# Combine weights transposed four tiles at a time and spread to their rows by DMA, S's columns made in pairs: an attention, soft-MoE and MLP kernel

## The chip, the core and the metric

The kernel runs on one core of a Trainium2 chip. The metric is device time in microseconds (us) of one execution, lower is better. The engines are named as the profile names them: PE is the matmul engine, PEld its weight loads, DVE the vector engine, ACT the scalar engine, POOL GpSimd, SP the engine whose queue issues the DMAs.

## The reference

Three layers follow each other, all in float32. What is computed, cut to what matters:

```python
# 1 attention: q, k, v are 8 batches x 8 heads x 576 x 64; keys and values are averaged in groups of 8 (72 left)
attn = softmax(q @ k_p.T / 8) ; x = (attn @ v_p), laid out as 4608 tokens x 512
# 2 soft MoE, 8 experts of 4 slots each (32 slots)
logits = x @ phi                               # 4608 x 32
d = softmax(logits, axis=0); slot_input = d.T @ x
slot_out[e] = relu(slot_input[e] @ w1[e]) @ w2[e]   # w1 512x1024, w2 1024x512 per expert
c = softmax(logits, axis=1)                    # the combine weights
y = c @ slot_out                               # 4608 x 512
# 3 MLP
g = s * relu(y @ w_in) ** 2 + b                # w_in 512 x 2048
out = g @ w_out                                # w_out 2048 x 512
```

The w_in and w_out that arrive are 64-bit floats, which the kernel turns into float32 itself.

## The kernel before

The program is one straight line of instructions per engine, in the order in which the source issues them. No engine overtakes its own queue, and waits are set by the data. SP issues every DMA, also in order.

**Attention, 0 to about 200 us.** The 36 tiles of 128 tokens pass through a hand-written pipeline. Its end leaves the logits in four tiles `L_t[pr]`, one for each pair of batches, 128 tokens x (9 tiles of tokens + 2 spare) x 32 slots.

**Experts, about 202 to 250 us.** A loop over `EORD` takes the 32 weight pieces of 1 MB (numbered 0 to 31 here; the loop's `n_`): w1 pieces write `l1` (L944), w2 pieces write `so_ps` (L952), each with 8 narrow matmul passes. After the last w1 piece of a half (pieces 7 and 21) `hidden` copies `l1` to SBUF on ACT (first half) and DVE (second half, L922), PE sums it one piece later (`hps`, L926), and ACT makes `h1z` from it (L928), which the w2 pieces read. `done(key, keep)` gives a piece's buffer back, or keeps it as scratch, and `pump` issues the next loads, strictly in the order of `loads`. `WIPOS` and `WOPOS` say ahead of which piece the first load of w_in and of w_out stands in that order; those two go to a `raw` buffer.

After each piece `step_convs` advances the generators in `convs` by one step and starts one more from `todo`. In `todo` stand:

- `combine(pr)`, the softmax over slots, in place in `L_t[pr]`;
- 20 `combine_t(pr, t0, n)`, which make the combine weights' transpose `cT` for two tiles of tokens (or one): ACT and DVE write the weights twice as a rounded high part and a low part into `cs`, PE transposes (L903), ACT copies to `cT`. A tile of `cT` has 128 rows: 32 slots x (high, low, high, low) parts;
- the first conversions: `conv_wi(0)`, `conv_wi(1)`, `conv_wo(0)`, `conv_wo(1)`. Each converts a 128 x 512 block by `narrow`: five DVE operations (L823 to L833), one on ACT (L835), two on POOL (L836, L837).

**The start of the MLP.** After piece 31, PE runs two filler matmuls on `cT` (`busy`, L980), the slots' outputs are transposed (`sot`), and a list `OPS` makes the first two column blocks of S = slot_out @ w_in (`s_a` writes `sps`, `s_b` spreads it to `Sw_t[f]` as high and low parts), the first hidden tiles (`st_h`, L1021), and their parts `gh` and `gl` (`st_g`). For step 0 both halves of `gh` are cast on DVE (L1048).

**The MLP, about 258 to 697 us.** 96 steps, each with 18 matmuls of 128 x 512 (`st_o`, L1078) and 2 of 128 x 384 (`st_h`). Conversions and, for f = 2 to 15, one `s_a` and one `s_b` each are threaded in between.

Of the kernel before, what the change touches and what calls it, by code (L numbers as in the profile page):

```python
# [56 lines left out]
def kernel(  # L57
# [793 lines left out]
    def s_a(f, ps):  # L851

        t = t_wi.pop(f)
        for kc in range(4):
# [1 line left out]
        sps = cv.tile([128, 128], F32, tag="sps", name="sps", bufs=2)
        sps_t[f] = sps
        nc.scalar.copy(out=sps, in_=ps[:, 0:128])

    def s_b(f, ps):  # L860

        nc.tensor.matmul(out=ps, lhsT=selrep.rearrange("p r s -> p (r s)"), rhs=sps_t.pop(f), start=True, stop=True)
        nc.scalar.copy(out=Sw_t[f], in_=ps)
        nc.vector.tensor_tensor(out=Sw_t[f][64:128], in0=ps[64:128], in1=Sw_t[f][64:128].bitcast(F32), op=ALU.subtract)  # L864
# [29 lines left out]
    def combine_t(pr, t0, n):  # L894
        cs = cv.tile([128, 2, 2, 2, 32], F32R, tag="cs", name="cs", bufs=2)[:, 0:n]
        cb = L_t[pr][:, 1 + t0:1 + t0 + n].unsqueeze(2).to_broadcast([128, n, 2, 32])
        nc.scalar.copy(out=cs[:, :, :, 0, :], in_=cb)
        nc.vector.tensor_tensor(out=cs[:, :, :, 1, :], in0=cb, in1=cs[:, :, :, 0, :].bitcast(F32), op=ALU.subtract)
        yield
        yield  # L900
        ps = ps_x.tile([128, 512], F32, tag="sx", name="ct")
        for i in range(n):
            nc.tensor.transpose(  # L903
                out=ps[:, 128 * i:128 * i + 128],
                in_=cs[:, i].rearrange("p a b s -> p (a b s)").bitcast(F32),
                identity=ident,
            )
# [295 lines left out]
```

## Time and profile before

| | |
|---|---|
| median of 3 runs | 707.07 us (705.78 to 707.13) |
| the profiled execution | 707.28 us |
| its span, first to last instruction | 705.2 us |
| PE busy | 661.7 us (94%) |
| DVE, ACT, POOL busy | 489.2, 410.2, 291.5 us |
| mean granted TensorE clock | 0.973 |
| DMA | 88.87 MB |

The profiled execution lies 0.21 us above the median and 2.1 us above its own span. The shares are averages over stages with different limits, so a stage is to be read in its own window: from 300 us on PE is busy in nearly every microsecond at a granted clock of 1.00; between 200 and 262 us the clock moves between 0.50 and 1.00 and other engines end PE's waits.

### The profile page before, as it was taken

Reading aid. Unit: us, or ns where it says so; the run is one execution under the profiler, and the core shown is the slowest. Engines: PE = TensorE matmul, PEld = TensorE weight load, DVE = VectorE, ACT = ScalarE, POOL = GpSimd, SP = SyncE. Lnnn points to the kernel's source line nnn. Section 1 sums busy time; section 2 is a strip of 40 time slices with the busy share of each in tenths; the row PEclk is TensorE's granted clock in tenths of the full one; section 3 lists DMA queues with packets and bytes.
Section 4 is the critical chain, followed back from the end, with each engine's and each line's share of the span. In section 5 each row is a group of like instructions: output and inputs, shape, how many; then the busy total and the mean of one; then the engine's idle time right before and its main releaser. Section 6 shows DMA issues by size and latency. Waiting matters only on the chain.

```text
span 705.2 us, 11293 instructions
## 1 busy us (share of the span) xinstructions
PE 661.7 (94%) x4354; PEld 518.3 (73%) x4354; DVE 489.2 (69%) x771; ACT 410.2 (58%) x714; POOL 291.5 (41%) x221
## 2 busy tenths in 40 slices
PE   7777989898989879999999999999999999999997
PEld 6665768677743348778888878788788788888885
DVE  6879777677582686888667788886765674556443
ACT  3664666665323347885666656666565666555552
POOL 3866466422100353543243335444141433999000
PEclk9998999999689989999999999999999999999999
DMA  8999276626669931011030110301100000222222
GB/s 290 383 344 311 109 240 241 239 72 229 248 237 384 361 142 61 1 59 60 2 118 2 60 59 1 119 1 61 60 0 1 1 0 1 89 91 88 92 91 89
DMA packets 41317, 88.87 MB, mean 126 GB/s; under 512 B 6960, under 2 KB 15152, under 8 KB 41264
## 3 DMA queue, kind: packets, MB, share of 16 engines
q1 hardware_dynamic: 41264, 88.16, 36.1%
q8 instruction: 34, 0.56, 0.3%
q14 instruction: 19, 0.16, 0.1%
HBM read 78.71 MB, written 9.44 MB: 125 GB/s over the span
## 4 chain that ended last, share of the span: by engine, by line
PE 77%; DVE 14%; ACT 4%; issue 1%; DMA 1%; POOL 1%; SPq 1%; DVEq 0%; ACTq 0%; POOLq 0%
PE o L1078 53%; PE h L1021 5%; PE sc L389 3%; PE l L944 3%; DVE S L398 2%; DVE mx L396 2%; PE so_ps L952 2%; DVE sm L407 2%; PE w L440 1%; DMA ring<-in_q_dram 1%; PE w L606 1%; ACT S L406 1%; PE w L359 1%; PE w L583 1%; PE ct L903 1%
## 5 line engine op out<-in xcount | busy, mean ns | idle before, releaser
L1078 PE MATMUL o<-whi,gh 128*128 128x512 f32 x576 | 229.1, 398 | 2.5 <-DVE gh L1048 2.5
L1078 PE MATMUL o<-whi,gl 128*128 128x512 f32 x576 | 225.1, 391 | 1.0 <-DVE gl L1049 1.0
L1078 PE MATMUL o<-wlo,gh 128*128 128x512 f32 x576 | 225.2, 391 | 0.0
L1030 ACT ACTIVATE r<-h 128x768 f32<-128x768 f32 x95 | 77.2, 813 | 151.9 <-PE h L1021 148.0
L1049 DVE TENSOR_TENSOR gl<-r,gh 128x768 fp32r<-128x768 f32 (+1 forms) x97 | 114.5, 1181 | 63.2 <-ACT gh L1038 62.8
L1091 DVE SCALAR_TENSOR_TENSOR part<-o,sb_t,part 128x512 f32<-128x512 f32 x144 | 99.6, 744 | 50.3 <-PE o L1078 47.8
L1078 PEld LDWEIGHTS o<-whi,gh 128*128 128x128 f32 x576 | 108.6, 188 | 23.9 <-issue 5.6
L1078 PEld LDWEIGHTS o<-wlo,gh 128*128 128x128 f32 x576 | 108.4, 188 | 24.0
L1078 PEld LDWEIGHTS o<-whi,gl 128*128 128x128 f32 x576 | 108.7, 189 | 21.6 <-DVE gl L1049 2.9
L836 POOL TENSOR_TENSOR fr<-fr,xp 128x512 f32<-128x512 f32 x28 | 41.0, 1464 | 182.4 <-ACT fr L835 160.3
L1031 ACT ACTIVATE r<-r 128x768 f32<-128x768 f32 x95 | 80.4, 847 | 3.0
L1038 ACT CAST gh<-r 128x768 fp32r<-128x768 f32 x95 | 79.5, 837 | 2.4
L427 POOL TENSOR_TENSOR P<-S,rs 128x576 f32<-128x576 f32 x32 | 37.3, 1166 | 72.7 <-DVE rs L410 38.0
L1172 POOL TENSOR_TENSOR part<-part,wsum 128x512 f32<-128x512 f32 x36 | 53.3, 1521 | 10.5 <-ACT wsum L1166 10.5
L1021 PE MATMUL h<-cT,S 128*128 128x384 f32 x192 | 48.8, 336 | 0.5 <-DVE S L864 0.5
L837 POOL TENSOR_TENSOR th<-th,fr 128x512 f32<-128x512 f32 x28 | 43.0, 1537 | 2.2
L1021 PEld LDWEIGHTS h<-cT,S 128*128 128x128 f32 x192 | 35.9, 188 | 8.1 <-DVE S L864 0.7
L407 DVE TENSOR_REDUCE sm<-S 128x8 f32<-128x584 f32 x36 | 27.3, 758 | 19.8 <-ACT S L406 19.7
L389 PE MATMUL sc<-kb,qT 128*128 128x144 f32 x256 | 39.7, 301 | 0.2 <-ACT qT L361 0.2
L396 DVE TENSOR_REDUCE mx<-sc 128x8 f32<-128x576 f32 x36 | 26.4, 734 | 15.5 <-PE sc L389 12.9
L389 PEld LDWEIGHTS sc<-kb,qT 128*128 128x128 f32 x256 | 35.5, 201 | 0.7 <-ACT qT L361 0.5
L406 ACT ACTIVATE S<-S 128x576 f32<-128x576 f32 x36 | 24.6, 682 | 19.5 <-DVE S L398 19.2
(211 smaller groups left out, 899.4 us busy)
## 6 DMA issues: line engine op xcount, KB each, us to landing
ring<-in_moe_w_dram SPq DMA_DIRECT2D x14, 1024.0 KB, 7.3
x<-in_moe_w_dram SPq DMA_DIRECT2D x13, 1024.0 KB, 9.2
raw<-in_moe_w_in_dram SPq DMA_DIRECT2D x8, 1024.0 KB, 5.5
raw<-in_moe_w_out_dram SPq DMA_DIRECT2D x8, 1024.0 KB, 4.8
out_dram<-part SPq DMA_DIRECT2D x32, 256.0 KB, 2.5
ring<-in_q_dram SPq DMA_DIRECT2D x7, 1024.0 KB, 13.4
ring<-in_v_dram SPq DMA_DIRECT2D x9, 768.0 KB, 11.4
ring<-in_k_dram SPq DMA_DIRECT2D x7, 768.0 KB, 7.7
```

The costliest lines, as they stand in the source:

```text
L389: nc.tensor.matmul(out=sc[:, i // 2, 2 * KP * (i % 2):2 * KP * (i % 2) + 2 * KP], lhsT=qT[:, i, :], rhs=kb[:, H * bb + 4 * (j % 2) + i, :] ...
L407: nc.vector.tensor_reduce(out=sm, in_=S, axis=AX.X, op=ALU.add)
L836: nc.gpsimd.tensor_tensor(out=fr, in0=fr, in1=xp, op=ALU.mult)
L837: nc.gpsimd.tensor_tensor(out=th if dst is None else dst, in0=th, in1=fr, op=ALU.add)
L1021: nc.tensor.matmul(out=h[x][:, 0:384] if i == 0 else h[:, x, 0:384], lhsT=Sw_t[f], rhs=cT(c, 384), start=True, stop=True)
L1030: nc.scalar.activation(out=r, in_=h[:, :, 0:384], func=ACTF.Relu)
L1031: nc.scalar.activation(out=r, in_=r, func=ACTF.Square)
L1038: nc.scalar.copy(out=gh_t[i], in_=r)
L1049: nc.vector.tensor_tensor(out=gl[:, x], in0=r[:, x], in1=gh[:, x].bitcast(F32), op=ALU.subtract)
L1078: nc.tensor.matmul(out=o_t[tt], lhsT=l[:, x, 128 * c:128 * c + 128], rhs=r, start=(fi == 0 and n == 0), stop=(fi == GROUPS[g] - 1 and n == 2),
L1091: nc.vector.scalar_tensor_tensor(out=p, in0=o_t[tt], scalar=sb_t[:, 0:1], in1=p, op0=ALU.mult, op1=ALU.add)
L1172: nc.gpsimd.tensor_tensor(out=p, in0=p, in1=wsum, op=ALU.add)
```

## The change

- The four tiles of logits become one, `L_all`, 128 x 11 x 4 x 32, so that for one index of a tile of tokens the four pairs' 32 slots lie side by side: 128 columns. `L_t[pr]` is now a strided view of it.
- `combine_t` is one generator. It transposes the nine blocks of 128 columns in groups of 4, 4 and 1; ACT writes the rounded high part back in place into `L_all`, DVE writes the low part into a fourth kept buffer, `kept[3]`. Then 16 DMAs of 32 rows x 1152 columns carry, for each pair, high, low, high, low to the four row groups of `cT`.
- It is started at piece 15, the first conversions at pieces 18, 19, 23 and 24 (table `BEHIND`). `WIPOS` goes from 22 to 25, `WOPOS` from 25 to 26. A fourth buffer is kept, and three of the four (pieces 7, 8, 9) from earlier pieces than before.
- S's columns are made for two f at a time where both are converted (`ready`): `s_a` and `s_b` take a pair, with one copy, one matmul of 256 columns, one cast and one subtract. f = 4 and f = 7, the last of groups of three, stay single, and so do f = 0 and 1.
- For step 0 the first half of `gh` is cast on ACT, the second on DVE. `wsum`'s first two steps come after both `wlo`.

```diff
-WIPOS, WOPOS = 22, 25
+WIPOS, WOPOS = 25, 26
+BEHIND = {15: "c", 18: "i0", 19: "i1", 23: "o0", 24: "o1"}
...
-    L_t = [cpool.tile([128, 11, 32], F32, name=f"L{i}") for i in range(NPR)]
+    L_all = cpool.tile([128, 11, NPR, 32], F32, name="L")
+    L_t = [L_all[:, :, i, :] for i in range(NPR)]
...
-    def s_a(f, ps):
-
-        t = t_wi.pop(f)
-        for kc in range(4):
-            nc.tensor.matmul(out=ps[32 * kc:32 * kc + 32, 0:128], lhsT=sot[:, kc, :], rhs=t[:, kc, :], start=True, stop=True)
...
+    def s_a(fs, ps):
+
+        for i, f in enumerate(fs):
+            t = t_wi.pop(f)
+            for kc in range(4):
+                nc.tensor.matmul(
+                    out=ps[32 * kc:32 * kc + 32, 128 * i:128 * i + 128], lhsT=sot[:, kc, :], rhs=t[:, kc, :], start=True, stop=True
+                )
+        n = 128 * len(fs)
...
+        nc.scalar.copy(out=sps_t[fs[0]], in_=ps[:, 0:n])
+
+    def s_b(fs, ps):
+
+        n, f = 128 * len(fs), fs[0]
+        nc.tensor.matmul(out=ps[:, 0:n], lhsT=selrep.rearrange("p r s -> p (r s)"), rhs=sps_t.pop(f), start=True, stop=True)
...
-    def combine_t(pr, t0, n):
-        cs = cv.tile([128, 2, 2, 2, 32], F32R, tag="cs", name="cs", bufs=2)[:, 0:n]
...
+    def combine_t():
+
+
+        x0 = 0
+        for j0, n in ((0, 4), (4, 4), (8, 1)):
+            x = 128 * n
+            Lc = L_all[:, 1 + j0:1 + j0 + n].rearrange("p j r s -> p (j r s)")
+            ps = ps_x.tile([128, 512], F32, tag="sx", name="ct")
+            for i in range(n):
+                nc.tensor.transpose(out=ps[:, 128 * i:128 * i + 128], in_=Lc[:, 128 * i:128 * i + 128], identity=ident)
+            nc.scalar.copy(out=Lc.bitcast(F32R), in_=ps[:, 0:x])
+            yield
+            nc.vector.tensor_tensor(out=kept[3][:, x0:x0 + x].bitcast(F32R), in0=ps[:, 0:x], in1=Lc, op=ALU.subtract)
+            x0 += x
+        hl = (L_all[:, 1:10].rearrange("p j r s -> p (j r s)"), kept[3][:, 0:x0])
+        for pr in range(NPR):
+            dst = cT(9 * pr * 128, x0).bitcast(F32)
+            for r in range(4):
+                nc.sync.dma_start(out=dst[32 * r:32 * r + 32], in_=hl[r % 2][32 * pr:32 * pr + 32])
...
-        done(key, 3 if n_ > 9 else int(n_ > 2))
+        done(key, 4 if n_ > 6 else int(n_ > 2))
...
+        if n_ in BEHIND:
+            x, f = BEHIND[n_][0], int(BEHIND[n_][1:] or 0)
+            todo.appendleft(conv_wi(f) if x == "i" else islice(wo_[f], 2) if x == "o" else combine_t())
...
+        if i == 0:
+            nc.scalar.copy(out=gh[:, 0], in_=r[:, 0])
+            nc.vector.tensor_copy(out=gh[:, 1], in_=r[:, 1])
         for x in (slice(0, 1), slice(1, 2)) if i == 0 else (slice(0, 2),):
-            if i == 0:
-                nc.vector.tensor_copy(out=gh[:, x], in_=r[:, x])
             nc.vector.tensor_tensor(out=gl[:, x], in0=r[:, x], in1=gh[:, x].bitcast(F32), op=ALU.subtract)
...
+    def ready():
+
+        if not t_wi:
+            return ()
+        f = min(t_wi)
+        g, i = GOF[f]
+        if i + 1 == GROUPS[g]:
+            return (f,)
+        return (f, f + 1) if f + 1 in t_wi else ()
```

Three places where instructions change their order. First DVE's queue around piece 21. `cs` are the old high and low parts, L the logits, `si_all` the copy of `l1` that `hps` needs, and `ring<-raw` is the start of a conversion. Before:

```order
L922 COPY si_all<-l_2654 128x512
L898 TENSOR_TENSOR cs<-L_75,cs 128x4x32 x2
L823 TENSOR_SCALAR ring_86<-raw_65 128x512
L824 TENSOR_SCALAR ring_86<-ring_86 128x512
L825 TENSOR_SCALAR ring_86<-ring_86 128x512
L829 SCALAR_TENSOR_TENSOR ring_84<-raw_65,ring_86 128x512
L833 TENSOR_SCALAR ring_86<-ring_84 128x512
```

And DVE's queue at the same place now, where `ring_79` is the kept buffer of the low part:

```order
L917 TENSOR_TENSOR ring_79<-ct,L 128x128
L826 TENSOR_SCALAR ring_78<-raw_65 128x512
L827 TENSOR_SCALAR ring_78<-ring_78 128x512
L828 TENSOR_SCALAR ring_78<-ring_78 128x512
L832 SCALAR_TENSOR_TENSOR ring_80<-raw_65,ring_78 128x512
L836 TENSOR_SCALAR ring_78<-ring_80 128x512
L826 TENSOR_SCALAR ring_78<-raw_65 128x512
L827 TENSOR_SCALAR ring_78<-ring_78 128x512
L828 TENSOR_SCALAR ring_78<-ring_78 128x512
L832 SCALAR_TENSOR_TENSOR ring_80<-raw_65,ring_78 128x512
L836 TENSOR_SCALAR ring_78<-ring_80 128x512
L935 COPY si_all<-l_2648 128x512
```

The copy for the second `hps` stood ahead of all conversions, and now stands behind the first two.

Next SP's queue of loads after piece 4 (`brief`), before; `moe_w2` are expert pieces, `moe2_w_in` and `moe2_w_out` the MLP's weights:

```order
L136 DMA brief_2639<-in_moe_w1_dram 128x2x1024
L136 DMA raw0_65<-in_moe2_w_in_dram 128x4x512
L136 DMA ring7_86<-in_moe_w2_dram 128x4x512
L136 DMA ring6_85<-in_moe_w2_dram 128x4x512
L136 DMA ring1_80<-in_moe_w2_dram 128x4x512
L136 DMA raw2_67<-in_moe2_w_out_dram 128x2x1024
```

And SP's queue from the same load on now:

```order
L140 DMA brief_2633<-in_moe_w1_dram 128x2x1024
L140 DMA ring7_83<-in_moe_w2_dram 128x4x512
L140 DMA ring6_82<-in_moe_w2_dram 128x4x512
L140 DMA ring1_77<-in_moe_w2_dram 128x4x512
L140 DMA raw0_65<-in_moe2_w_in_dram 128x4x512
L140 DMA raw2_67<-in_moe_w2_dram 128x4x512
L140 DMA raw1_66<-in_moe2_w_out_dram 128x2x1024
```

The three pieces that go to ring buffers now stand ahead of the w_in load, which waits for a raw buffer. The order after piece 31's load, now, is the start of the 16 new DMAs, with the next w_in load behind the last of them:

```order
L140 DMA x_2403<-in_moe_w2_dram 128x4x512
L923 DMA cT0_2629<-L_72 32x1152
L923 DMA cT0_2629<-ring3_79 32x1152
L923 DMA cT0_2629<-L_72 32x1152
L923 DMA cT0_2629<-ring3_79 32x1152
L923 DMA cT0_2629<-L_72 32x1152
```

The first four carry pair 0, which is all that `busy` and steps 0 and 1 read of `cT`; the transposes before wrote `cT` from ACT, with no DMA.

## Rows read from the trace of the kernel before

**Rows 1.** The page's part 4: shares of the chain that ended last, by line.

```profile
PE o L1078 53%; PE h L1021 5%; PE sc L389 3%; PE l L944 3%; DVE S L398 2%; DVE mx L396 2%; PE so_ps L952 2%; DVE sm L407 2%; PE w L440 1%; DMA ring<-in_q_dram 1%; PE w L606 1%; ACT S L406 1%; PE w L359 1%; PE w L583 1%; PE ct L903 1%
```

**Rows 2.** The chain of waits in the experts' stage: start us, us, what.

```profile
201.80 8.73 PE l L944 x56
210.53 0.37 PE ct L903 x2
210.90 1.00 PE l L944 x8
...
213.26 1.90 PE hps L926 x16
...
217.77 0.26 PE ct L903
```

**Rows 3.** PE's timeline, 243 to 259 us: start, us, instructions [idle before, releaser].

```profile
243.90 0.33 PE L903 MATMUL ct<-ident,cs 128*128 128x128 f32 x1 [2.37 <-DVE cs L898]
244.16 1.70 PE L952 MATMUL so_ps<-raw,ring 128*32 128x512 f32 x8
245.61 3.89 PE L952 MATMUL so_ps<-x,ring 128*32 128x512 f32 x24
...
251.73 0.64 PE L855 MATMUL o<-ring,sot 128*32 128x128 f32 x16 [0.45 <-ACT sot L990]
...
258.01 0.73 PE L1078 MATMUL o<-whi,gl 128*128 128x512 f32 x1 [0.32 <-DVE gl L1049]
```

**Rows 4.** Windows: us, busy of PE, PEld, DVE, ACT, POOL, PEclk, DMA share, GB/s.

```profile
206.00:210.00 4.00, 4.00 (x40) 1.20 (x32) 3.79 (x11) 0.86 (x4) 1.06 (x1) 0.89 0.00 0
212.00:243.00 31.00, 29.50 (x225) 10.20 (x224) 11.69 (x27) 12.06 (x41) 2.71 (x2) 1.00 1.04 388
243.00:248.00 5.00, 4.10 (x21) 1.17 (x25) 4.83 (x8) 1.54 (x3) 2.77 (x2) 0.66 0.89 298
```

**Rows 5.** DVE's timeline: the first operation of each of the four conversions.

```profile
236.84 0.42 DVE L823 TENSOR_SCALAR ring<-raw 128x512 uint32<-128x512 uint32 x1
...
239.28 0.42 DVE L823 TENSOR_SCALAR ring<-raw 128x512 uint32<-128x512 uint32 x1
...
243.76 0.42 DVE L823 TENSOR_SCALAR ring<-raw 128x512 uint32<-128x512 uint32 x1
...
248.12 0.42 DVE L823 TENSOR_SCALAR ring<-raw 128x512 uint32<-128x512 uint32 x1
```

**Rows 6.** POOL's timeline: its first operation beside the third conversion.

```profile
243.89 1.43 POOL L836 TENSOR_TENSOR ring<-ring 128x512 f32<-128x512 f32 x1 [1.18 <-DVE cs L898]
```

**Rows 7.** DVE's timeline: the copy ahead of the second hps.

```profile
232.57 0.69 DVE L922 COPY si_all<-l 128x512 f32<-128x512 f32 x1 [0.27 <-PE l L944]
```

**Rows 8.** DVE's timeline ahead of step 0.

```profile
255.66 1.42 DVE L1048 CAST gh<-r 128x384 fp32r<-128x384 f32 x1
257.12 0.84 DVE L1049 TENSOR_TENSOR gl<-r,gh 128x384 fp32r<-128x384 f32 x1
```

**Rows 9.** DVE's timeline: gl of both halves with POOL idle.

```profile
280.02 0.96 DVE L1049 TENSOR_TENSOR gl<-r,gh 128x768 fp32r<-128x768 f32 x1 [0.73 <-ACT gh L1038]
```

**Rows 10.** The chain of waits in the MLP: a step without and one with S.

```profile
267.23 4.10 PE o L1078 x18
...
271.68 1.38 PE o L1078 x6
273.06 0.36 PE h L855 x8
...
274.31 0.22 PE h L862 x2
...
276.96 1.15 PE o L1078 x5
```

**Rows 11.** DMA issues by line, 500 to 705 us: KB each, median us from issue to landing.

```profile
out_dram<-part SPq DMA_DIRECT2D x32, 256.0 KB, 2.5
out_dram<-part SPq DMA_DIRECT2D x8, 128.0 KB, 2.4
```

More of the change, by code (lines that the diff above doesn't have):

```diff
@@ L231 @@
         nc.gpsimd.memset(kb_t[i], 0.0)
-    for i in range(NPR):
-        nc.gpsimd.memset(L_t[i], -3.0e38)
+    nc.gpsimd.memset(L_all, -3.0e38)
     S_buf = [sc2.tile([128, 2, 4, KP + 1], F32, name=f"S{i}", bufs=1) for i in range(2)]
@@ L849, in conv_wi @@
         t_wi[f] = t
-    def s_a(f, ps):
-        t = t_wi.pop(f)
-        for kc in range(4):
-            nc.tensor.matmul(out=ps[32 * kc:32 * kc + 32, 0:128], lhsT=sot[:, kc, :], rhs=t[:, kc, :], start=True, stop=True)
[L856 to L864, printed above, removed]
+    def s_a(fs, ps):
[6 more added lines that the diff above has]
+        n = 128 * len(fs)
+        c0 = 128 if fs[0] == 1 else 0
+        sps_t[fs[0]] = sps[:, c0:c0 + n]
+        nc.scalar.copy(out=sps_t[fs[0]], in_=ps[:, 0:n])
+    def s_b(fs, ps):
+        n, f = 128 * len(fs), fs[0]
+        nc.tensor.matmul(out=ps[:, 0:n], lhsT=selrep.rearrange("p r s -> p (r s)"), rhs=sps_t.pop(f), start=True, stop=True)
+        S = Sw.rearrange("p f x -> p (f x)")[:, 128 * f:128 * f + n]
+        nc.scalar.copy(out=S, in_=ps[:, 0:n])
+        nc.vector.tensor_tensor(out=S[64:128], in0=ps[64:128, 0:n], in1=S[64:128].bitcast(F32), op=ALU.subtract)
     def conv_wo(f):
@@ L892, in step_convs @@
             next(convs[-1])
-    def combine_t(pr, t0, n):
-        cs = cv.tile([128, 2, 2, 2, 32], F32R, tag="cs", name="cs", bufs=2)[:, 0:n]
[L896 to L907, printed above, removed]
-        c0 = (9 * pr + t0) * 128
-        nc.scalar.copy(out=cT(c0, 128 * n), in_=ps[:, 0:128 * n])
+    def combine_t():
[7 more added lines that the diff above has]
+            nc.scalar.copy(out=Lc.bitcast(F32R), in_=ps[:, 0:x])
+            yield
+            nc.vector.tensor_tensor(out=kept[3][:, x0:x0 + x].bitcast(F32R), in0=ps[:, 0:x], in1=Lc, op=ALU.subtract)
[5 more added lines that the diff above has]
+                nc.sync.dma_start(out=dst[32 * r:32 * r + 32], in_=hl[r % 2][32 * pr:32 * pr + 32])
     so_ps = ps_1.tile([128, 512], F32, tag="so", name="so_ps")
@@ L1000 @@
     wsum = wp.tile([128, DM], F32, name="wsum")
-    Sw_t = [wp.tile([128, 128], F32R, name=f"S{f}") for f in range(NF)]
+    sps = wp.tile([128, 256], F32, name="sps")
+    Sw = wp.tile([128, NF, 128], F32R, name="S")
     fp2 = ctx.enter_context(tc.tile_pool(name="fp2", bufs=2, side="right"))
@@ L1118 @@
             next(wo_[n], None)
+    for gen in wo_:
+        next(gen, None)
     rctx.close()
```

20 lines of the change are left out of this document (8 added, 12 removed).

## The prediction

> **What bounds the kernel now.** I read the chain of waits first, as shares by line, then its pieces in order of time, then the timelines of the engines at the places that the change touches. The shares [rows 1] show where the end is made: 53% lies on the output matmuls L1078 and 5% on L1021, the MLP's 96 steps. There a step without S takes 4.45 us (267.23 to 271.68) and one with S 5.28 us (to 276.96) [rows 10]; nothing but matmuls stands between. So the MLP is bound by PE's own work, and what S adds, 0.83 us each, is paid in full 14 times: 11.6 us.
>
> The experts' stage, 201.8 to 249.5 us, is the other place. Its chain is PE again: seven pieces to 210.53 without transposes, then one piece of 1.00 us after another with transposes between them, 0.37 us for two and 0.26 us for one, and 1.90 us for each `hps` [rows 2]. Near its end a last transpose waits 2.37 us for `cs`, which DVE makes only after two conversions, and the four pieces behind it take 5.27 us, 244.23 to 249.50, in place of 4.0 [rows 3], because the granted clock of that stretch is 0.66 (a mix of the 1.2 and 2.4 GHz levels), where it was 1.00 before the wait [rows 4]. DMA runs at 388 GB/s from 212 to 243 us after lying idle from 206 to 210 [rows 4].
>
> **Part 1: transposes out of the experts' stage.** Away go 20 groups, 16 of two and 4 of one: 16 x 0.37 + 4 x 0.26 = 7.0 us at most [rows 2]. One transpose takes 0.26 us and each further 0.11, so the new groups of 4, 4 and 1 take 0.59 + 0.59 + 0.26 = 1.44 us. The wait of 2.37 us goes, since no transpose stands behind a conversion any more, and with it the slow clock, 1.27 us. I walk PE's new order instead of adding these: from 210.53, 25 pieces x 1.00 + 2 x 1.90 + 1.44 = 240.8 us for the end of piece 31, against 249.5. That is 8.7 us if nothing new waits.
>
> Does DMA keep up? The last 12 loads (10 pieces, w_in, w_out) can now start at about 205.6, where the traffic of before ends, because the three pieces at their head need only buffers that PE freed. Twelve times 1.05 MB at 388 GB/s is 32.4 us, so piece 31 lands near 238 to 239 and is wanted at 239.8. That is covered, by about one us.
>
> **Part 2: a new wait.** DVE's queue now holds, ahead of the copy for the second `hps`, the third low part and two whole conversions. By the walk, piece 15 ends at 221.4 and the third transpose group at 224.9; ACT's cast and DVE's subtract bring the start of the first conversion to 225.5. One conversion takes DVE 2.44 us while POOL is idle (236.84 to 239.28) and 4.36 us while POOL works on the one before (243.76 to 248.12) [rows 5, 6]. So the second ends at 225.5 + 2.44 + 4.36 = 232.3 and the copy, 0.69 us [rows 7], at 233.0. PE reaches `hps` at 229.9 and can do the half that ACT's copy feeds, 0.95 us; it then stands idle from 230.8 to 233.0, 2.2 us. Queued behind it are the rest of `hps` and the last nine pieces. An idle of 2.37 us was followed by the slow stretch above [rows 3, 4], so I add its 1.27 us. Bounds: 0 if the second conversion isn't slowed, which gives 0.3 us of wait and no loss of clock, up to 3.5. I take 3.5, since the row that matches the overlap is the 4.36. Piece 31 then ends at 244.3: 5.2 us earlier than before.
>
> **Part 3: cT by DMA.** The 16 DMAs of 147 KB stand in SP's queue behind all the loads. The two filler matmuls wait for the first four, 0.59 MB: 1.5 us at 388 GB/s behind piece 31's load, so 240.3, and with the 2.4 us that a transfer of 128 KB needs from issue to landing [rows 11] counted on top at most 242.7. PE wants them at 244.3, so they cost nothing, with 1.6 us to spare; behind that wait stand the transposes of `so` and everything after. The other twelve are read from step 2's hidden tile on, more than 10 us later. The next w_in load moves behind them, from 243.3 to about 244 or 245, and its conversion isn't due before 254: hidden, and late only if SP is held up by 5 us more. No row shows a transfer from SBUF to SBUF; bounds are 0 and, at a quarter of the rate, 6.0 us + 2.4 from 238.8, thus 247.2, a cost of 2.9. I take 0.
>
> The trace's rows for half as many partitions and bytes (2.4 us) and for all (2.5 us) [rows 11] show hardly a gain from halving. The Trainium skill, SBUF — State Buffer, section "Door 1: The DMA port swizzle", says that a transfer's bandwidth depends on how many of 16 ports its partitions reach, and 32 adjacent ones reach eight. By that rule each new DMA would go at half the rate, the four would be done 1.5 us later, and the sum would stay as it is while the case without the new wait (below) would lose 1 to 2 us.
>
> **Part 4: the start of the MLP.** The chain there passes through DVE's cast of the first half of `gh` (1.42 us) and its `gl` (0.84 us), with POOL busy beside both [rows 8]. Now the first `gh` is ACT's, while DVE casts the second, and POOL has done its conversions, since they began 11 us earlier. `gl` of 768 columns takes 0.96 us with POOL idle [rows 9], half of it about 0.48. After the square at 255.7 (old times) the cast of a half takes about as long, 0.48, then `gl` 0.48, so the second matmul starts at 256.7 in place of 258.0 [rows 3]: 1.3 us. Bounds: 0 to 1.5.
>
> **Part 5: pairs.** Six pairs take the place of twelve single S steps. In a pair the second `s_a` adds eight passes: 0.36 us if they cost what eight cost alone [rows 10], about 0.2 if they flow as in the run of 16 in 0.64 us [rows 3]. `s_b`'s matmul of 256 columns costs between the 0.22 us of 128 columns [rows 10] and twice that. So a pair costs 0.83 + 0.2 + 0.1 = 1.13 us, between 1.03 and 1.41, in place of 1.66. I take 0.53 saved, six times: 3.2 us, with bounds 1.5 and 3.8. The wider copies on ACT and DVE sit in their idle time.
>
> Edits at nothing: the combine's operations on strided logits (off the chain from 202 to 211 us, first read at 221), the single memset, the ready order of `wsum`. If the strided writes cost 0.1 us in each of 20 reductions of the attention stage, that is at most 2 us, and I put that in the range.
>
> **The sum.** 5.2 + 1.3 + 3.2 = 9.7 us. From the profiled execution's 707.28, which is 0.21 above the median, that gives 697.6.
>
> **The rivals.**
> *No new wait (or a short one).* DVE runs the second conversion at 2.44 us, or the clock holds through an idle of 2.2 us. For it: a conversion without POOL beside it does take 2.44. Against it: POOL's first operation starts as soon as the first conversion's are done. Gain 8.7 + 1.3 + 3.2 = 13.2, less up to 1.9 where PE, now at 240.8, waits for the cT transfers until 242.7: 694.1 to 696.0; I say 694.6.
>
> *cT comes late.* PE stands at the fillers because the transfers go at a fraction of the rate, or because SP, which issues them in order, reaches them late. At a quarter of the rate the cost was 2.9 us above: 700.5. For it: no row shows such a transfer. Against it: they need to be 1.6 us later than the worst of my counts before they cost anything.
>
> *Slower than before.* The same place, at a far lower rate: the first four must land after 244.3 + 9.7 + 1.4 = 255.4, 16.6 us after the loads, which for 0.59 MB is 36 GB/s, a tenth of the rate of [rows 4]. From there each us counts in full; at 30 GB/s they land at 258.5: 710.4. Nothing in the trace points there.
>
> *The pairs bring nothing.* The single step's cost is in the passes, and a pair costs two singles: the sum loses 3.2, 700.8. Against it: the run of 16 passes in 0.64 us.
>
> **How the numbers follow.** Forecast 0.52; no or a short new wait 0.21; cT late by a few us 0.12; pairs without gain 0.08; slower 0.04; nothing gained because some part undoes another 0.03. The range runs from 693.6 (the second case with pairs at 3.8) to 702.0 (cT late, with pairs at the weak bound): it leaves out under 0.2. About 0.2% (1.4 us) is what a measurement of this kernel can tell from no change. Faster by more than that: 0.93; within it: 0.03; slower: 0.04.
>
> **What would show it.** Right: piece 31's end near 244, one idle of about 2 us inside the second `hps` put down to DVE's copy, a granted clock under 1 behind it, the first output matmuls near 251, S steps of about 5.6 us for two f. Wrong, step by step: no idle at that `hps` (part 2); PE idle ahead of the fillers, put down to a DMA (part 3); idle ahead of a w2 or w1 piece put down to its load (part 1's DMA count); the cast of `gh` still ending PE's wait (part 4); steps with a pair above 6.1 us (part 5). The whole prediction falls if the granted clock in the MLP drops for stretches that before ran at 1.00.

## The result and the profile after

The changed kernel took 698.52 us (median of 4 runs, 694.91 to 699.83) beside 707.10 us before (4 runs, 705.78 to 707.66); the ratio is 0.9862 with a 95% interval of 0.9836 to 0.9888, thus 8.6 us less. The forecast was 697.6 with a range of 693.6 to 702.0. Measured again later (the run a2_after_again below) the ratio was 0.9898, interval 0.9865 to 0.9930. The size came out near the forecast, but in the profiled execution one of its three terms was too large by 1.8 us, one too small by 2.1 and one too large by 1.1, and in the second trace they came out otherwise again. The profiled execution took 698.94 us, its span is 697.1.

The chain that ended last, from the page, answers to [rows 1]: the output matmuls keep their share, and two DMAs stand in it that stood nowhere before.

```profile
PE 74%; DVE 14%; DMA 4%; ACT 4%; SPq 2%; issue 1%; POOL 0%; DVEq 0%; ACTq 0%
PE o L1092 52%; PE h L1034 4%; PE sc L392 3%; PE l L957 2%; DVE S L401 2%; DVE mx L399 2%; DMA cT<-ring 2%; DVE sm L410 2%; PE w L443 1%; DMA ring<-in_q_dram 1%; ACT S L409 1%; PE w L609 1%; DMA raw<-in_moe_w_in_dram 1%; PE w L362 1%; PE w L586 1%
```

PE's timeline from the second `hps` to the third hidden tile (start, us, instructions, idle before and its releaser) answers to [rows 3]. Lines have moved: w2 pieces are L965, fillers L992, hidden tiles L1034, output matmuls L1092.

```profile
229.00 1.08 PE L939 MATMUL hps<-sel,si_all 128*128 128x32 f32 x8
232.74 1.92 PE L939 MATMUL hps<-sel,si_all 128*128 128x32 f32 x8 [2.66 <-DVE si_all L935]
...
242.76 1.03 PE L965 MATMUL so_ps<-x,ring 128*32 128x512 f32 x8
245.50 1.07 PE L965 MATMUL so_ps<-x,ring 128*32 128x512 f32 x8 [1.71 <-DMA x<-in_moe_w_dram]
246.82 0.73 PE L992 MATMUL l<-cT 128*128 128x512 f32 x2 [0.25 <-DMA cT<-ring]
...
252.99 0.50 PE L1092 MATMUL o<-whi,gh 128*128 128x512 f32 x1 [1.14 <-ACT gh L1060]
253.59 0.50 PE L1092 MATMUL o<-whi,gl 128*128 128x512 f32 x1
...
256.21 0.51 PE L1034 MATMUL h<-cT,S 128*128 128x384 f32 x2
```

Two long waits are to be seen: the forecast one for DVE's copy (2.66 us, forecast 2.2), and one that the sum had left out, 1.71 us for the load of piece 31. The windows (us; busy of PE, PEld, DVE, ACT, POOL; granted clock; DMA share; GB/s) show what goes with each, and answer to [rows 4]:

```profile
228.00:230.00 2.00, 2.00 (x20) 1.10 (x12) 1.93 (x3) 0.59 (x1) 1.92 (x2) 1.00 1.05 388
230.00:232.00 2.00, 0.08 (x1) 0.00 (x0) 1.93 (x3) 0.00 (x0) 0.61 (x1) 0.85 1.05 389
232.00:234.00 2.00, 1.26 (x6) 1.26 (x7) 1.97 (x4) 0.00 (x0) 1.67 (x2) 0.50 1.03 383
...
238.00:240.00 2.00, 2.00 (x24) 0.51 (x20) 1.97 (x2) 0.06 (x1) 1.92 (x2) 0.94 1.10 354
240.00:242.00 2.00, 2.00 (x24) 0.57 (x20) 1.24 (x2) 0.00 (x0) 0.85 (x2) 1.00 1.06 235
242.00:244.00 2.00, 1.79 (x20) 0.27 (x12) 0.00 (x0) 0.00 (x0) 1.92 (x2) 1.00 0.88 195
```

Behind the idle the granted clock is 0.50, the 1.2 GHz level, until 238. And from 240 on DMA is as busy as before but moves half: 195 to 235 GB/s in place of 388. The DMA issues (KB each, us from issue to landing) of the last load and of the first and the fourth cT transfer:

```profile
x<-in_moe_w_dram SPq DMA_DIRECT2D x1, 1024.0 KB, 16.6
cT<-L SPq DMA_DIRECT2D x1, 144.0 KB, 14.2
cT<-ring SPq DMA_DIRECT2D x1, 144.0 KB, 11.4
```

The fourth cT transfer was issued at 235.35 and landed at 246.8, where I had put it at 242.7 at most.

In the MLP the chain shows a step with a pair: from one hidden tile to the next, 274.58 to 280.27, it takes 5.69 us, beside 4.45 without S and 5.28 with a single column [rows 10].

```profile
274.58 0.35 PE h L1034 x2
274.93 1.38 PE o L1092 x6
276.31 0.57 PE h L859 x16
276.88 0.90 PE o L1092 x3
277.79 0.43 PE h L870 x2
278.22 2.05 PE o L1092 x9
280.27 0.36 PE h L1034 x2
```

Where the 8.1 us between the two spans went is read from four marks of PE's timeline, here with the same marks of all kernels that were run. "Fillers" is the start of the two matmuls behind piece 31 (L980, now L992); "third hidden tile" is the one made in step 0; "last" is the start of the last output matmul. The ratio is to the kernel before, run beside each.

| kernel | first w1 | fillers | third hidden tile | last | fillers to third tile | third tile to last | ratio (95%) |
|---|---|---|---|---|---|---|---|
| before | 201.80 | 249.43 | 262.24 | 699.93 | 12.81 | 437.69 | 1 |
| changed | 202.60 | 246.82 | 256.21 | 691.81 | 9.39 | 435.60 | 0.9862 (0.9836 to 0.9888) |
| a2_after_again | 201.73 | 247.16 | 258.90 | 694.11 | 11.74 | 435.21 | 0.9898 (0.9865 to 0.9930) |
| e1_singles | 202.77 | 245.46 | 256.37 | 694.10 | 10.91 | 437.73 | 0.9928 (0.9904 to 0.9952) |
| e2_twelve_later | 202.70 | 246.64 | 259.04 | 694.30 | 12.40 | 435.26 | 0.9911 (0.9890 to 0.9931) |
| e3_copy_first | 202.84 | 247.79 | 261.53 | 696.89 | 13.74 | 435.36 | 0.9912 (0.9880 to 0.9944) |
| e4_cast_on_dve | 202.62 | 246.47 | 256.61 | 691.82 | 10.14 | 435.21 | 0.9887 (0.9862 to 0.9912) |
| e5_strided | 202.82 | 249.64 | 262.30 | 700.03 | 12.66 | 437.73 | 1.0009 (0.9991 to 1.0026) |
| e6_all_behind | 201.62 | 251.93 | 264.68 | 699.93 | 12.75 | 435.25 | 1.0029 (1.0010 to 1.0049) |
| e7_reordered | 202.19 | 247.10 | 260.84 | 696.27 | 13.74 | 435.43 | 0.9959 (0.9941 to 0.9977) |
| e8_brief7 | 203.58 | 246.28 | 258.55 | 694.14 | 12.27 | 435.59 | 0.9878 (0.9855 to 0.9901) |
| e9_order | 203.21 | 245.37 | 256.31 | 691.53 | 10.94 | 435.22 | 0.9857 (0.9835 to 0.9879) |
| e12_with_fillers | 202.42 | 244.97 | 254.34 | 689.79 | 9.37 | 435.45 | 0.9857 (0.9836 to 0.9879) |
| e13_late_conversions | 203.15 | 245.54 | 259.28 | 694.65 | 13.74 | 435.37 | 0.9903 (0.9873 to 0.9932) |

Changed against before: the experts' stage starts 0.8 us later and is 3.4 us shorter, the stretch from the fillers to the third hidden tile is 3.4 us shorter, the rest 2.1. In the second trace of the same kernel (a2_after_again) the three are 2.2, 1.1 and 2.5 us: each row of the table is one execution, and the same work can take some us more or less in it.

### The profile page after: what moved, and what is told of

Its sections match the earlier page's. It is cut to its first block, busy times and chain, and to the rows that moved or that the text cites. A ratio compares the mean times of both kernels' runs of the same rounds, so it can differ in the third digit from the quotient of the medians.

```text
span 697.1 us, 11173 instructions
## 1 busy us (share of the span) xinstructions
PE 652.3 (94%) x4315; PEld 516.8 (74%) x4315; DVE 481.8 (69%) x747; ACT 400.1 (57%) x666; POOL 290.5 (42%) x218
## 4 chain that ended last, share of the span: by engine, by line
PE 74%; DVE 14%; DMA 4%; ACT 4%; SPq 2%; issue 1%; POOL 0%; DVEq 0%; ACTq 0%
PE o L1092 52%; PE h L1034 4%; PE sc L392 3%; PE l L957 2%; DVE S L401 2%; DVE mx L399 2%; DMA cT<-ring 2%; DVE sm L410 2%; PE w L443 1%; DMA ring<-in_q_dram 1%; ACT S L409 1%; PE w L609 1%; DMA raw<-in_moe_w_in_dram 1%; PE w L362 1%; PE w L586 1%
## 5 line engine op out<-in xcount | busy, mean ns | idle before, releaser
L1092 PE MATMUL o<-whi,gh 128*128 128x512 f32 x576 | 227.9, 396 | 1.1 <-ACT gh L1060 1.1
L1092 PE MATMUL o<-whi,gl 128*128 128x512 f32 x576 | 224.9, 391 | 0.9 <-DVE gl L1063 0.7
L1092 PE MATMUL o<-wlo,gh 128*128 128x512 f32 x576 | 224.6, 391 | 0.0
L1092 PEld LDWEIGHTS o<-wlo,gh 128*128 128x128 f32 x576 | 108.2, 188 | 23.5
L1092 PEld LDWEIGHTS o<-whi,gl 128*128 128x128 f32 x576 | 108.3, 188 | 22.5 <-DVE gl L1063 3.5
L1092 PEld LDWEIGHTS o<-whi,gh 128*128 128x128 f32 x576 | 108.2, 188 | 21.7 <-issue 1.8
L1034 PE MATMUL h<-cT,S 128*128 128x384 f32 x192 | 48.8, 336 | 0.5 <-DVE S L873 0.5
L1034 PEld LDWEIGHTS h<-cT,S 128*128 128x128 f32 x192 | 36.0, 188 | 8.0 <-DVE S L873 0.7
```

The lines of the kernel that those rows point to most:

```text
L1034: nc.tensor.matmul(out=h[x][:, 0:384] if i == 0 else h[:, x, 0:384], lhsT=Sw[:, f, :], rhs=cT(c, 384), start=True, stop=True)
L1092: nc.tensor.matmul(out=o_t[tt], lhsT=l[:, x, 128 * c:128 * c + 128], rhs=r, start=(fi == 0 and n == 0), stop=(fi == GROUPS[g] - 1 and n == 2),
```

## The experiments

My theory was now: the cT transfers hold the last load up, so the stage ends when DMA is done, and PE's wait at `hps` costs nothing. The rivals: the load is late by its own queue; or the wait at `hps` is what costs, as the prediction had it.

**The wait at hps taken away.** The second conversion starts three pieces later, behind DVE's copy.

```diff
-BEHIND = {15: "c", 18: "i0", 19: "i1", 23: "o0", 24: "o1"}
+BEHIND = {15: "c", 18: "i0", 22: "i1", 23: "o0", 24: "o1"}
```

> The changed kernel with the second conversion moved behind DVE's copy for the second hidden transposes (the new wait of part 2). PE should no longer stand 2.66 us ahead of that half of hps, nor run at half the clock behind it. Theory A (the wait is worth the 3.5 us of my prediction): 3.0 to 3.5 us shorter, about 695. Theory B (the load of piece 31 lands at 245.4 whatever PE does, and takes the wait's place): PE waits 4.5 to 5.5 us for that load, piece 31 ends at 246.6 as before, and with a slow clock behind that idle the time is between the changed kernel's and 1.5 us more, 698.5 to 700. I expect B.

PE's timeline and two windows of this kernel:

```profile
229.44 1.97 PE L939 MATMUL hps<-sel,si_all 128*128 128x32 f32 x16
...
241.58 1.93 PE L965 MATMUL so_ps<-x,ring 128*32 128x512 f32 x8 [2.43 <-DMA x<-in_moe_w_dram]
245.93 1.94 PE L965 MATMUL so_ps<-x,ring 128*32 128x512 f32 x8 [2.41 <-DMA x<-in_moe_w_dram]
```

```profile
229.00:240.00 11.00, 8.97 (x80) 3.37 (x72) 10.66 (x14) 2.52 (x5) 7.20 (x6) 1.00 1.05 384
240.00:262.00 22.00, 16.59 (x64) 10.04 (x65) 8.76 (x14) 6.91 (x14) 7.46 (x7) 0.53 0.83 233
```

`hps` runs through and the clock holds at 1.00, but PE then waits 2.43 and 2.41 us for the last two loads, and the clock is 0.53 for the 22 us behind that. The ratio, 0.9912, is no better than the changed kernel's on the same chip (0.9898). Theory B holds in its main point: the wait is not worth its 3.5 us, because the loads end the stage. From the first w1 matmul to the fillers it takes 44.95 us here, beside 44.22 and 45.43 in the two traces of the changed kernel.

**The cT transfers out of the last load's way.** All 16 are issued behind the next two w_in loads and a w_out load; `rows_to`, which issues those of the pairs that it is given, is called behind the loop over the pieces.

```diff
-        for pr in range(NPR):
+        rows_to(hl, 0, 0)
...
     assert not todo, len(todo)
+    rows_to(late[0], 0, NPR)
```

> The changed kernel with all 16 cT transfers moved behind the next two w_in loads and a w_out load in SP's queue, so that nothing but loads follows the last piece's load. Theory (the cT transfers beside its last packets hold that load up): DMA keeps its 388 GB/s through 240, the last load lands by 240.5, PE doesn't wait for it, and instead waits for the cT transfers at the fillers until 250 or later: 4 to 9 us longer than the changed kernel. Rival (the load comes late by its own queue, whatever follows it): it lands at 243.5 to 245.8 as in the four traces so far, with DMA at about 388 GB/s until then.

```profile
238.00:240.00 2.00, 2.00 (x24) 0.58 (x20) 1.47 (x3) 0.00 (x0) 0.38 (x2) 1.00 1.05 389
240.00:242.00 2.00, 2.00 (x20) 0.36 (x12) 0.00 (x0) 0.00 (x0) 1.92 (x2) 1.00 1.05 386
242.00:244.00 2.00, 0.01 (x4) 0.00 (x0) 0.00 (x0) 0.58 (x1) 0.31 (x1) 1.00 1.05 392
246.00:248.00 2.00, 0.00 (x0) 0.00 (x0) 0.00 (x0) 0.00 (x0) 0.00 (x0) 0.62 1.06 278
```

PE's last two pieces and the fillers, and the issue of the last load:

```profile
240.12 1.89 PE L972 MATMUL so_ps<-x,ring 128*32 128x512 f32 x16
251.93 1.19 PE L1000 MATMUL l<-cT 128*128 128x512 f32 x2 [9.91 <-DMA cT<-ring]
```

```profile
x<-in_moe_w_dram SPq DMA_DIRECT2D x1, 1024.0 KB, 14.2
```

DMA keeps 386 to 392 GB/s to 244, and PE ran both last pieces without a wait from 240.12 on. The last load was issued at 225.97 and landed 14.2 us later, at 240.2; in the changed kernel it was issued at 228.86 and landed 16.6 us later, at 245.4. In all ten traces with cT transfers issued right behind it, it takes 15.9 to 17.2 us. From 246, when the cT transfers run, the rate falls to 278 and then to 214 to 246. PE stood 9.91 us at the fillers for them, and the kernel was 1.3% slower than the changed one, 9.3 us, a little over what I had given it. The rival falls: without cT traffic beside it the load lands 2.4 us sooner after its issue, and PE doesn't wait for it. The other 2.9 us between the two landings are an earlier issue, 1.0 of them because the whole stage began earlier in this execution.

**Only the first four left in place.** The other 12 move to that later point.

```diff
-        for pr in range(NPR):
+        rows_to(hl, 0, 1)
...
     assert not todo, len(todo)
+    rows_to(late[0], 1, NPR)
```

> The changed kernel with 12 of the 16 cT transfers (those of pairs 1 to 3) moved behind the next w_in and w_out loads in SP's queue; the first four stay where they are. In the changed kernel's trace the last piece's load lands at 245.4, 5.5 us after the 239.9 that its bytes at 388 GB/s would give, in a stretch where DMA is fully busy but moves only 195 to 235 GB/s; PE waits 1.71 us for it and 0.25 us for the first four. Theory (the cT transfers run beside the tail of the load and take its rate): the wait for the last load goes or falls under 0.5 us, piece 31 ends near 244.8 in place of 246.6, and the following w_in load is no longer late (0.4 us in the fifth step): 1.8 to 2.4 us shorter, 696.1 to 696.7. Rival (the load is late because SP issued it late, at 231.4, and any load lands 14 us after its issue): PE still waits 1.5 to 2 us for it, and the time stays within 0.5 us of the changed kernel. Other side: pair 1's transfers, now behind three loads, land after the 256.2 at which the third step's hidden tile reads them, and PE waits there.

PE's last piece and the fillers:

```profile
244.59 1.06 PE L972 MATMUL so_ps<-x,ring 128*32 128x512 f32 x8 [1.06 <-DMA x<-in_moe_w_dram]
246.64 0.73 PE L1000 MATMUL l<-cT 128*128 128x512 f32 x2 [0.98 <-DMA cT<-ring]
```

PE still waited 1.06 us for the last load, which landed 16.1 us after its issue, and 0.98 for the first four; DMA moved 195 GB/s from 240 to 242. So the four alone are enough to hold the load up, and my expectation that the other 12 were needed for it falls. 0.9911 is no gain.

**What four of them cost.** An attempt at a better version: the first four ahead of the last two pieces' loads, four behind a w_in load, eight later, and the second conversion behind the copy.

```diff
-BEHIND = {15: "c", 18: "i0", 19: "i1", 23: "o0", 24: "o1"}
+BEHIND = {15: "c", 18: "i0", 22: "i1", 23: "o0", 24: "o1"}
...
+HELD = 30
...
+            if key in EORD[HELD:] and not t_ct:
+                return
...
-        for pr in range(NPR):
+        rows_to(hl, 0, 1)
+        t_ct.append(1)
+        pump()
...
+        if n_ == 24:
+            rows_to(late[0], 1, 2)
+        if n_ == 28:
+            rows_to(late[0], 2, NPR)
```

> An attempt at a better version from the two waits found: the second conversion stands behind DVE's copy (no wait at hps), the first four cT transfers stand ahead of the last two pieces' loads, the next four behind a w_in load, the last eight later. Theory: the first four cost the loads 2.5 to 3 us of DMA time, the last load lands at 242.5, PE, which is there at 239 to 240, waits 2.5 to 3 us for it, piece 31 ends near 243.7 in place of 246.6, and nothing waits at the fillers: 2 to 3 us shorter than the changed kernel if the clock holds. Rival (the idle at the last piece is followed by a stretch at the 1.2 GHz level, as the kernel with the copy first showed): the gain is eaten up, 0 within 1 us.

```profile
230.00:233.00 3.00, 2.54 (x23) 1.05 (x26) 2.86 (x6) 1.16 (x3) 0.59 (x2) 1.00 1.05 389
234.00:240.00 6.00, 3.73 (x36) 0.72 (x28) 5.83 (x7) 0.70 (x1) 4.22 (x4) 1.00 1.04 235
240.00:245.00 5.00, 1.94 (x8) 0.20 (x8) 0.98 (x2) 0.00 (x0) 2.53 (x2) 0.58 1.05 387
```

This prices the transfer that no row of before showed. In the 6 us from 234 DMA moved 1.41 MB, of which 0.59 MB is the four transfers; the other 0.82 MB would have taken 2.1 us at 389 GB/s. Four transfers thus take 3.9 us from the loads, where I had counted 1.5. PE waited 3.71 us for piece 30 and 0.77 for piece 31, and the granted clock was 0.58 there. The ratio puts this kernel 0.6%, 4.3 us, behind the changed one: both of my expectations missed. The trace shows the loss behind the stage: the fillers start at 247.10, as in a2_after_again, but from there to the third hidden tile it takes 13.74 us beside 9.39 and 11.74.

**Neighbours in the queue on different halves of the partitions.**

The question was whether neighbours on different halves move faster together.

```diff
-            for r in range(4):
+            for r in (0, 2, 1, 3):
```

> The changed kernel with the four cT transfers of a pair issued in the order 0, 2, 1, 3 of their 32-row groups, so that neighbours in the queue go to different halves of the 128 partitions. With the order 0, 1, 2, 3 DMA is fully busy from 240 on but moves only 177 to 235 GB/s, where loads move 388. [...] Rival (each transfer by itself is slow, or its source, always 32 neighbouring rows, sets the rate): 180 to 240 GB/s as before and the time within 0.5 us of the changed kernel.

```profile
240.00:242.00 2.00, 2.00 (x24) 0.51 (x20) 1.93 (x3) 0.00 (x0) 0.84 (x1) 1.00 1.07 246
242.00:244.00 2.00, 1.94 (x21) 0.36 (x13) 0.31 (x1) 0.00 (x0) 1.46 (x2) 1.00 0.96 228
248.00:250.00 2.00, 1.34 (x9) 1.14 (x8) 0.52 (x2) 0.96 (x5) 1.14 (x1) 1.00 1.01 221
```

In these windows, with DMA nearly fully busy, the rate is 221 to 246 GB/s: this order brings nothing back. Whether each transfer is slow by itself, or its source sets the rate (32 neighbouring rows in both orders), this doesn't tell. The ratio, 0.9857, is close to that of the changed kernel's first measurement; I don't put it down to the edit.

**Part 4 undone.** Both halves of the first `gh` are cast on DVE again.

```diff
-            nc.scalar.copy(out=gh[:, 0], in_=r[:, 0])
-            nc.vector.tensor_copy(out=gh[:, 1], in_=r[:, 1])
+            pass
         for x in (slice(0, 1), slice(1, 2)) if i == 0 else (slice(0, 2),):
+            if i == 0:
+                nc.vector.tensor_copy(out=gh[:, x], in_=r[:, x])
```

> The changed kernel with part 4 undone: DVE makes both halves of the first gh again, each just ahead of its gl. The changed kernel's trace has an idle of 1.14 us ahead of the first output matmul and full clock behind it; the kernel before had 2.50 us there, 0.32 more ahead of the second, and a granted clock of 0.53 to 0.62 from 258 to 262, in which the first step took 1.6 us more. Theory A (the cast sets the wait, and the longer idle brings the slow clock): the second output matmul 1 to 1.5 us later and the first step 1.6 us longer: 2.5 to 3.1 us longer than the changed kernel, about 701. Theory B (only the wait, since POOL is idle there now and the casts are short): 0.5 to 1.5 us longer and full clock.

DVE's two casts and POOL's operation that starts between them:

```profile
252.57 0.35 DVE L1063 CAST gh<-r 128x384 fp32r<-128x384 f32 x1
253.44 1.45 DVE L1063 CAST gh<-r 128x384 fp32r<-128x384 f32 x1
```

```profile
252.96 1.71 POOL L888 TENSOR_TENSOR wlo<-ring,whi 128x512 fp32r<-128x512 f32 x1 [2.36 <-ACT whi L886]
```

The same cast takes 0.35 us with POOL idle and 1.45 with POOL at work. The second output matmul starts 7.10 us after the fillers, 6.77 in the changed kernel and 8.58 before: of the 1.8 us gained there 0.3 goes with ACT's cast, and I put the other 1.5 down to POOL's being done earlier, which no run changes alone. The ratio of 0.9887 shows no loss; both theories gave too much.

**The conversions late again.** To show the same from the other side.

```diff
-BEHIND = {15: "c", 18: "i0", 19: "i1", 23: "o0", 24: "o1"}
+BEHIND = {15: "c", 25: "i0", 26: "i1", 27: "o0", 28: "o1"}
```

> The changed kernel with its four conversions started at pieces 25 to 28, late as in the kernel before, so that POOL still works on them when the first gh is made; the cast of the first half stays on ACT and nothing else is changed. In the changed kernel the second output matmul starts 6.77 us after the fillers (8.58 in the kernel before, 7.10 with both casts on DVE), and DVE's cast of half a gh takes 0.36 us with POOL idle beside it and 1.42 to 1.45 with POOL busy. Theory (the gain at the start of the MLP is that POOL's conversions are over, and ACT's cast adds only 0.3): DVE's cast takes about 1.4 us again and the second output matmul starts 8.0 to 8.6 us after the fillers. Rival (the gain is ACT's cast, which takes the first half off DVE): 6.8 to 7.2. For the whole, the wait at hps goes, since DVE's copy stands ahead of the conversions, and a wait of 4 to 6 us for the last pieces' loads takes its place; with the later start 1 to 3 us longer than the changed kernel, ratio 0.989 to 0.993.

It does not tell the two apart: DVE had finished the four conversions by 245.0, the cast took 0.36 us as in the changed kernel, and the second output matmul, 8.88 us after the fillers, stood in a stretch at a granted clock of 0.53 (242 to 260). What it does show is the first experiment once more: no wait at `hps`, 0.85 and 3.39 us for the last two loads instead, fillers at 245.54, and a ratio of 0.9903. From the first w1 matmul to the fillers it takes 42.39 us; the kernels with the wait at `hps` and the transfers in place take 42.16 to 45.43.

**Part 5 undone.** S's columns one at a time.

```diff
-        return (f, f + 1) if f + 1 in t_wi else ()
+        return (f,)
```

> The changed kernel with part 5 undone: S's columns are made one f at a time again, in 14 steps. In the changed kernel's trace a step with a pair takes 5.69 us, one with a single 5.28 and one without 4.45, so a pair costs 1.24 where two singles cost 1.66. Theory (pairs save matmul passes, and the MLP is bound by PE): 6 x 0.42 = 2.5 us longer than the changed kernel, about 701; my prediction's term was 3.2, so 701.7. Rival (pairs bring nothing, because the passes are the cost): no longer than the changed kernel, 698.5 within 0.5. The first output matmul should start at the same time within 0.5 us in either case.

From the third hidden tile on it takes 437.73 us, within 0.04 of the kernel before, beside 435.21 to 435.60 in all kernels with pairs: 2.1 to 2.5 us. The ratio is 0.0030 above the changed kernel's on the same chip, 2.1 us; the two intervals overlap, so the marks decide, and the rival falls by them. The first output matmul, which I had expected within 0.5 us of the changed kernel's, started 1.4 us earlier, at 251.58.

**The strided logits alone**, in the kernel before.

```diff
-    L_t = [cpool.tile([128, 11, 32], F32, name=f"L{i}") for i in range(NPR)]
+    L_all = cpool.tile([128, 11, NPR, 32], F32, name="L")
+    L_t = [L_all[:, :, i, :] for i in range(NPR)]
...
-    for i in range(NPR):
-        nc.gpsimd.memset(L_t[i], -3.0e38)
+    nc.gpsimd.memset(L_all, -3.0e38)
```

> The kernel before with one edit alone: the logits of all pairs in one tile, so that the attention stage writes and reads them with a stride. The first w1 matmul starts at 201.80 us in the kernel before and at 202.60 in the changed one. My prediction put this edit at nothing, with up to 2 us in its range. Theory (the stride or the single memset costs): first w1 matmul at 202.5 to 202.8 and 0.8 us longer than the kernel before. Rival (the 0.8 us is a difference between executions, from loads that land a little later): it starts at 201.8 within 0.3, and the ratio is 1.000 within 0.002.

The time is the same, 1.0009 (0.9991 to 1.0026). The first w1 matmul is at 202.82, but kernels with the same stride start it anywhere from 201.62 to 203.58, so the 0.8 us of the first trace is within what executions differ by.

**The changed kernel again.**

> The changed kernel itself once more, as the reference for the other kernels that run beside it, and to see how far its waits move from one execution to the next: the ratio to the kernel before should lie at 0.986 within 0.003. What the runs so far leave open is the wait ahead of the last piece (1.71 us in its first trace, 0.27 and 0 in two kernels with the same loads and transfers): if it comes from the order in which the DMA engines finish, it moves between 0 and 2 us here too.

```profile
210.62 1.93 PE L957 MATMUL l<-brief,siz 128*32 128x512 f32 x8 [2.68 <-DMA brief<-in_moe_w_dram]
236.24 1.08 PE L939 MATMUL hps<-sel,si_all 128*128 128x32 f32 x8 [2.67 <-DVE si_all L935]
```

Here PE waited for the fifth piece, not for the last: its load (`brief`) took 9.7 us from issue to landing, 6.9 in the first trace, 4.7 in the kernel before, where nothing is loaded behind it. PE came to the last piece later and found it and the transfers there. The fillers start at 247.16 all the same. The ratio, 0.9898, lies just outside the 0.983 to 0.989 that I had expected. The stretch from the fillers to the third hidden tile, 9.39 us in the first trace, takes 11.74 here: the granted clock falls to 0.50 again, from about 251 to 258.

```profile
250.00:252.00 2.00, 1.34 (x12) 1.00 (x6) 0.52 (x2) 0.93 (x4) 1.27 (x1) 0.83 1.01 219
252.00:254.00 2.00, 1.28 (x5) 0.78 (x4) 1.36 (x3) 1.69 (x4) 0.00 (x0) 0.50 0.90 192
```

**The fifth piece's load wanted later**: that piece stands eighth in the order.

```diff
-    BRIEF = 4
+    BRIEF = 7
```

> The changed kernel with the piece that is loaded into the space of the attention stage (tile brief) used as the eighth instead of the fifth, so that its load is wanted 3 us later. In both kernels without the new transfers it lands 4.7 and 5.8 us after its issue and PE doesn't wait; in eight traces of the changed kernel and its variants it lands 5.9 to 9.7 us after, and PE waits up to 2.7 us for it, because three more loads run beside it. Theory: that wait is gone, no other takes its place before the second hps, and the median is 0.5 to 1.5 us shorter than the changed kernel's (ratio to before 0.986 to 0.988, where the changed kernel showed 0.986 and 0.990). Rival: the experts' stage ends when its last load and the cT transfers land, whatever PE waits for earlier, so the time is the same within 0.5 us and the wait comes back at the last piece.

The wait is gone and comes back as 0.42 us for the last load and 0.47 for cT. 0.9878 beside 0.9898 is 1.4 us less, with intervals that overlap: unclear.

**The edits of e8_brief7 and e9_order together, and fillers behind the first hidden tiles.** The new part:

```diff
-OPS = "o0 a0 o0 a1 b0 b1 h0 g0 o1 h1 o1 g1"
+OPS = "o0 a0 o0 a1 b0 b1 h0 w4 g0 o1 h1 o1 g1"
```

> The two edits above together, and four filler matmuls behind the first two hidden tiles, where PE stands 0.7 to 1.1 us idle until the first gh. Theory (the stretch at half the clock in the first step, 1.6 us in the kernel before and in some traces of the changed one, follows such idles): the first output matmul starts no later, the first step runs at full clock, and with the other two edits the median is 1.5 to 3 us shorter than the changed kernel's, ratio 0.983 to 0.986. Rival (the clock there follows the longer waits before it, at hps and at the last piece): a half-clock stretch still falls between 232 and 262 us in the trace, and the gain is that of the two other edits alone, 0 to 1.5 us.

```profile
248.98 0.62 PE L1034 MATMUL h<-cT,S 128*128 128x384 f32 x2 [0.46 <-DVE S L873]
249.43 1.09 PE L992 MATMUL o<-cT 128*128 128x512 f32 x4
250.36 0.51 PE L1034 MATMUL h<-cT,S 128*128 128x384 f32 x2
251.10 0.49 PE L1092 MATMUL o<-whi,gh 128*128 128x512 f32 x1 [0.23 <-ACT gh L1060]
```

The granted clock was 0.50 from 232 to 238 and 0.99 from there to 262. One trace can't tell whether the fillers did that, since the first trace of the changed kernel ran so without them. The ratio, 0.9857 (0.9836 to 0.9879), is the lowest, together with e9's, and not to be told from the changed kernel's 0.9862. No version was found that is better than the changed kernel beyond doubt.

## Why the prediction was right, point by point

**Part 1, right in what it removes, wrong in what it says of DMA.** The transposes are three groups. At full clock pieces with no transpose between them run about 0.86 us apart, where I had walked all of them at 1.00. "That is covered, by about one us" is the step that failed: piece 31's load landed at 245.4, not at 238 to 239. Only 2.4 us of this come from the cT transfers beside it: with the 14.2 us of e6_all_behind it would have landed at 243.1 (an estimate from the two traces), 4 to 5 us later than I had counted, so PE's walk without new waits, 240.8, would not have decided there. In the 11 traces in which the first four cT transfers stand beside the last loads the fillers start between 244.97 and 247.79, whatever PE waits for on the way: at `hps`, at the fifth piece or at the last two. In nine of them the last thing that PE waits for is the last load or the transfers; in a2_after_again and e4_cast_on_dve it came after both. So DMA bounds this stage in most executions of the changed kernel, not in all.

**Part 2, right in its mechanism, wrong in its price.** The wait is 2.66 us where I said 2.2, the conversion with POOL beside it 4.37 where I said 4.36, the clock behind it 0.50. But taking it away gained nothing (e3_copy_first, e13_late_conversions): behind it stood the loads.

**Part 3 is the term that was mis-sized.** I took 0 between 0 and 2.9. The first trace has 1.71 us for the last load and 0.25 for the four transfers, 1.96 in all. The size is that of one execution: in the six other traces with the wait at `hps` and all sixteen transfers in place (a2, e1, e4, e8, e9 and e12) the two come to 0 to 1.07 us. The row that I leaned on, 2.5 us for a transfer from issue to landing [rows 11], was of one that runs alone. I counted when the transfers would be done and not what they take from the loads in front of them: 3.9 us for four (e7_reordered). "cT comes late" was the rival that named the place. The next w_in load, which I had at 244 to 245, was issued at 252.0; the chain now passes through it, and the one step there that is longer, 4.87 us, puts 0.4 us on that at most.

The Trainium skill, SBUF — State Buffer, "Door 1: The DMA port swizzle", which I had weighed, has 32 neighbouring partitions reach eight of 16 ports, thus half the rate. The traces agree: 195 to 246 GB/s beside 388 in the windows shown. I had drawn from it only that the four are done 1.5 us later. The other half is in DMA: Bandwidth & Descriptors, "Two DMAs through the same engine are not ordered": nothing orders transfers across the 16 engines. The trace agrees: from 240 to 244, with the last load still under way until 245.4, the rate was already that of the slow transfers.

With parts 1 to 3 the stage came out 3.4 us shorter from first w1 to fillers, where I had 5.2.

**Part 4, right in its mechanism, but it left out the clock.** To the second output matmul 1.8 us were gained, where I had 1.3; the cast on ACT is 0.3 of it, and the rest goes with POOL's earlier end. What I did not count is that the first step before ran at a granted clock of 0.53 to 0.62 and in the first trace of the changed kernel at 1.00: 1.6 us more. The windows of the kernel before:

```profile
258.00:260.00 2.00, 1.99 (x5) 1.60 (x6) 1.97 (x2) 0.43 (x1) 2.00 (x2) 0.53 0.00 0
260.00:262.00 2.00, 2.00 (x7) 1.52 (x6) 2.00 (x3) 0.00 (x0) 0.46 (x1) 0.62 0.00 0
```

That this gain is the change's own is not shown: from the fillers to the third hidden tile, traces of the changed kernel and of kernels that do the same work there take 9.39 to 13.74 us, and the second trace of the changed kernel ran this step at 0.50 again.

**Part 5, right but high.** A pair costs 1.24 us, not 1.13, because `s_b` with 256 columns takes 0.43, the upper of my bounds (twice 0.22). Six pairs save 6 x (1.66 - 1.24) = 2.5 us; e1_singles measured 2.1 to 2.5. I had 3.2.

**The edits at nothing** were nothing (e5_strided). One thing I had overlooked: three loads now follow that of `brief` at once. It lands 5.1 to 9.7 us after its issue (4.7 and 5.8 without them), and in seven of the ten traces with the old order of pieces PE waits for it, 0.27 to 2.68 us. That those three loads are the cause was not tried by itself, and the two ranges overlap.

Of the places named beforehand, piece 31 ended at 246.6 (said: near 244), the first output matmul started at 252.99 (near 251) and a step with a pair took 5.69 us (about 5.6).

So 9.7 = 5.2 + 1.3 + 3.2 came out as 3.4 + 3.4 + 2.1, less 0.8 by which the first trace started the stage later: 8.1 us between the spans. The total came so near partly by luck: in that execution the clock gave what DMA took. The second trace has 2.2 + 1.1 + 2.5 = 5.8, and the second ratio, 0.9898, stands for 7.2 us, inside the stated range but 2.5 short of the forecast.

Three numbers beside the sum were off: for first transfers that land at 258.5 the kernel would take 697.6 + 14.2 = 711.8 us, not 710.4, and by their own terms the ends of the range are 693.5 and 702.2.

## What to carry to other kernels

Before work is moved from a busy engine to DMA, look at whether DMA is the next bound at that place, and charge the transfer with what it takes from the loads beside it, not only with its own landing. A wait that a trace shows is worth its length only if nothing else is due right behind it; here the loads were.
